# Thirty attention units as a hardware loop with hand-made semaphores, in a decode kernel that streams 572 MB

## The chip, the cores and the metric

The kernel runs on one core of a Trainium2 chip. The metric is device time in microseconds, the median of the runs shown. All other times come from one profiled execution of the same program, read as a page of tables and as answers from its trace.

## The reference

Two branches are computed for two tokens (B = 2, one position each) and mixed by a gate. Branch A is attention of one query over a cache of 16,384 positions in 32 heads of 128; branch B is an MLP with two layer norms. All inputs are bfloat16.

```python
x = A_x                                            # (2, 1, 1024)
g = sigmoid((x * gate_w).sum(-1, keepdims=True))
q = (x @ wq).reshape(B, 1, 32, 128).transpose(0, 2, 1, 3)     # wq: 1024 x 4096
p = softmax(einsum("bhqd,bhkd->bhqk", q, k_cache) * 128 ** -0.5)
a = (p @ v_cache).reshape(B, 1, 4096) @ wo                    # caches: 2 x 32 x 16384 x 128
h = gelu(layernorm(x) @ w1)                                   # w1, w2: 1024 x 1024
x1 = x + shifted(h) @ w2       # shifts along the one position: shifted(h) is zero
b = x1 + gelu(layernorm(x1) @ w3) @ w4                        # w3: 1024 x 3584, w4: 3584 x 1024
out = g * a + (1 - g) * b
```

## The kernel before

The caches are read once. One unit is two heads of one token: 8.39 MB of K and as much of V, each in one transfer of 128 rows of 64 KB. There are 32 units, numbered `n` or `u`; units 2i and 2i+1 are the two tokens of the same pair of heads. On-chip memory has one big tile `mem` of five cells of 32 KB per partition. K of even units lies in cells 0 and 1, K of odd units in cells 1 and 2, and V in cells 3 and 4. `wq`, then `w3`, then `w4` pass through cells 3 and 4 before the first V, and `w1` and `w2` through cell 2.

For each unit DVE transposes K in eight chunks (line 472). PE multiplies each chunk with the unit's query (line 478; 64 matmuls into one PSUM tile `S`). Then come the maximum (499 to 515; DVE, ACT and one PE matmul that brings the maxima to all partitions), the exponentials on ACT (517), and the sum and its reciprocal (531, 533). P.V is done two units later (553; 64 matmuls with 8 weight columns, which run on four groups of 32 rows of the result side by side), with DVE and two PE matmuls to reduce the four groups (569 to 609). After the second token of a pair the result is multiplied with two heads' rows of `wo` (441) into `arow`, a PSUM tile that stays open for the whole kernel.

All large loads go through SP's queue, in this order: `wq`, the two small inputs `xin` and `gwT`, `w1`, `w2`, K of unit 0, the two halves of `w3`, K of unit 1, then in each unit K of the next unit and V of the previous one, and every fourth unit two pairs' rows of `wo` (1 MB). K(n+1) is issued when the first half of unit n has been transposed, since the two share a cell; V(n-1) when P.V of unit n-2 has been read. The last V comes in nine pieces, the last rows of `wo` behind them. In the last units twelve tiny loads of a few rows (`probe`, line 456) go through the same queue.

The MLP and the query use their weights as the stationary operand: `LinearT.compute` (line 233) and line 268 issue one weight load and one matmul with two columns for each 128 x 128 block of a weight matrix: 256 for `wq`, 64 each for `w1` and `w2`, 224 each for `w3` and `w4`. The MLP's result is added into `arow` through 32 matmuls with the identity (line 402) and the output is copied from `arow` by DVE and ACT, a half each (688, 689).

The program is straight code for each engine. A scheduler orders the instructions and makes the semaphores.

Of the kernel before, what the change touches and what calls it, by code (L numbers as in the profile page):

```python
# [19 lines left out]
GELU_C1 = 0.044715  # L20


@with_exitstack
def kernel(
# [21 lines left out]
    assert D % P == 0 and F % P == 0 and H % 2 == 0  # L46
# [4 lines left out]

    HP = H // 2
    NU = HP * B
# [9 lines left out]
    assert NJ % CT == 0 and CT % GT == 0 and NG <= QP  # L63

    const = ctx.enter_context(tc.tile_pool(name="const", bufs=1))
    ktpool = ctx.enter_context(tc.tile_pool(name="ktpool", bufs=2))
    wopool = ctx.enter_context(tc.tile_pool(name="wopool", bufs=1))
    ppool = ctx.enter_context(tc.tile_pool(name="ppool", bufs=1))
    stat = ctx.enter_context(tc.tile_pool(name="stat", bufs=2))
    mlp = ctx.enter_context(tc.tile_pool(name="mlp", bufs=1))  # L70
    sps = ctx.enter_context(tc.tile_pool(name="sps", bufs=2, space=PSUM))
    ops = ctx.enter_context(tc.tile_pool(name="ops", bufs=1, space=PSUM))
    rps = ctx.enter_context(tc.tile_pool(name="rps", bufs=1, space=PSUM))
    mps = ctx.enter_context(tc.tile_pool(name="mps", bufs=2, space=PSUM))

    def misc_psum(shape, dtype=FP32):
        return mps.tile(shape, dtype, tag="misc", name="misc")


    mem = const.tile([P, 5 * CELL], BF16, name="mem")  # L80
# [3 lines left out]

    k_cell = [0 if u % 2 == 0 else 1 for u in range(NU)]
    v_cell = [3] * NU
    v_cell[NU - 2] = 0
    units = [(hp, b) for hp in range(HP) for b in range(B)]

    def cache_rows(cache, u):  # L90
        hp, b = units[u]
        return cache[b, 2 * hp : 2 * hp + 2].rearrange("h s d -> (h s) d").rearrange(
            "(p j) d -> p (j d)", p=P
        )

    def load_k(u):
        nc.sync.dma_start(out=region(k_cell[u], NJ * Dh), in_=cache_rows(A_k_cache, u))

    def load_v(u):
        nc.sync.dma_start(out=region(v_cell[u], NJ * Dh), in_=cache_rows(A_v_cache, u))  # L100

    def load_v_half(u, k):
        at = slice(k * CELL, (k + 1) * CELL)
        nc.sync.dma_start(out=region(v_cell[u], NJ * Dh)[:, at], in_=cache_rows(A_v_cache, u)[:, at])

    PIECES = [32] * 7 + [16] * 2
    assert sum(PIECES) == NJ

    def load_v_pieces(u):
        j = 0  # L110
        for n in PIECES:
            nc.sync.dma_start(
                out=region(v_cell[u], NJ * Dh)[:, j * Dh : (j + n) * Dh],
                in_=cache_rows(A_v_cache, u)[:, j * Dh : (j + n) * Dh],
            )
            j += n

    def k_view(u):
        return region(k_cell[u], NJ * Dh).rearrange("p (j d) -> p j d", d=Dh)

    def v_view(u):
        return region(v_cell[u], NJ * Dh).rearrange("p (j d) -> p j d", d=Dh)

    wq_t = region(3, KC * H * Dh).rearrange("p (r n) -> p r n", r=KC)
    nc.sync.dma_start(out=region(3, KC * H * Dh), in_=A_wq.rearrange("(p r) n -> p (r n)", p=P))
    xin = const.tile([P, B, KC], BF16)
    nc.sync.dma_start(out=xin[:], in_=A_x.rearrange("b s (p r) -> p (b s) r", p=P))
    gwT = const.tile([P, KC], BF16)
    nc.sync.dma_start(out=gwT[:], in_=gate_w.rearrange("(p r) -> p r", p=P))
    ident_f = const.tile([P, P], FP32)  # L130
    make_identity(nc, ident_f[:])
    ident_s = const.tile([P, P], FP32)
    nc.vector.tensor_scalar(
        out=ident_s[:], in0=ident_f[:], scalar1=-scale, scalar2=None, op0=ALU.mult
    )
    neg_half = const.tile([P, 1], FP32)
    nc.vector.memset(neg_half[:], -0.5)
    ones_f = const.tile([P, P], FP32)
    nc.vector.memset(ones_f[:], 1.0)

    sel = const.tile([P, 4, Q4, QP], BF16)
    nc.gpsimd.memset(sel[:], 0.0)
    for v in range(4):
        w, e = divmod(v, 2)
        nc.gpsimd.affine_select(
            out=sel[:, v],
            in_=sel[:, v],
            compare_op=ALU.not_equal,
            fill=1.0,
            base=-(2 * QP * w + e),  # L150
            pattern=[[0, Q4], [-2, QP]],
            channel_multiplier=1,
        )
    mask4 = const.tile([P, Q4], BF16)
    nc.gpsimd.memset(mask4[:], 1.0)
    nc.gpsimd.affine_select(
        out=mask4[:], in_=mask4[:], compare_op=ALU.is_ge, fill=0.0,
        base=0, pattern=[[-QP, Q4]], channel_multiplier=1,
    )
    nc.gpsimd.affine_select(  # L160
        out=mask4[:], in_=mask4[:], compare_op=ALU.is_ge, fill=0.0,
        base=QP - 1, pattern=[[QP, Q4]], channel_multiplier=-1,
    )

    hm2 = const.tile([P, 2], FP32)
    nc.vector.memset(hm2[:], 0.0)
    nc.vector.memset(hm2[0:HALF, 0:1], 1.0)
    nc.vector.memset(hm2[HALF:P, 1:2], 1.0)

    lmat = const.tile([P, P], FP32)  # L170
    nc.vector.tensor_copy(
        out=lmat[:].rearrange("p (g h k) -> p g h k", h=2, k=4),
        in_=hm2[:].unsqueeze(1).unsqueeze(3).to_broadcast([P, P // 8, 2, 4]),
    )

    sel8 = const.tile([P, 8], FP32)
    nc.vector.tensor_reduce(
        out=sel8[:],
        in_=ident_f[:].rearrange("p (c k) -> p k c", k=QP)[:, 0:8, :],
        axis=AX.X,  # L180
        op=ALU.add,
    )

    mask4m = const.tile([P, 4], FP32)
    nc.vector.tensor_tensor(out=mask4m[:], in0=sel8[:, 0:4], in1=sel8[:, 4:8], op=ALU.add)
    hsel = const.tile([P, 2], FP32)
    nc.vector.tensor_reduce(
        out=hsel[:], in_=sel8[:].rearrange("p (h k) -> p h k", k=4), axis=AX.X, op=ALU.add
    )
    oacc = [ops.tile([P, 4 * Dh], FP32, name=f"oacc{k}") for k in range(2)]  # L190
    for k in range(2):
        nc.vector.memset(oacc[k][:], 0.0)

    NW = 2
    WW = P + NG
    qw = []
    for k in range(NW):
        t = const.tile([P, 4, WW], BF16, name=f"qw{k}")
        nc.gpsimd.memset(t[:], 0.0)
        qw.append(t)  # L200
    NP = 4
    pts = []
    for k in range(NP):
        t = const.tile([P, NJ // 4, 2, 4], BF16, name=f"pt{k}")
        nc.gpsimd.memset(t[:], 0.0)
        pts.append(t)

    class LinearT:

        def __init__(self, W, actT, name, cell, offset, nparts=1):  # L210
            self.actT = actT
            K, self.N = W.shape
            self.R = K // P
            self.C = self.N // P
            self.rows = self.R // nparts
            self.src = W.rearrange("(p r) n -> p (r n)", p=P)

            self.at = [(cell + k) * CELL + offset for k in range(nparts)]
            self.acc = mlp.tile([P, self.C, B], FP32, name=f"{name}_acc")

        def part(self, k):
            return mem[:, self.at[k] : self.at[k] + self.rows * self.N]

        def load(self, k=0):
            n = self.rows * self.N
            nc.sync.dma_start(out=self.part(k), in_=self.src[:, k * n : (k + 1) * n])

        def compute(self, k, c0, c1):
            wc = self.part(k).rearrange("p (r n) -> p r n", n=self.N)
            ps = misc_psum([P, c1 - c0, B])  # L230
            for c in range(c0, c1):
                for r in range(self.rows):
                    nc.tensor.matmul(  # L233
                        ps[:, c - c0, :],
                        lhsT=wc[:, r, :].rearrange("p (m c) -> p c m", c=self.C)[:, c, :],
                        rhs=self.actT[:, k * self.rows + r, :],
                        start=(r == 0),
                        stop=(r == self.rows - 1),
                    )
            acc = self.acc[:, c0:c1, :]  # L240
            if k == 0:
                nc.vector.tensor_copy(out=acc, in_=ps[:])
            else:
                nc.vector.tensor_tensor(out=acc, in0=acc, in1=ps[:], op=ALU.add)

    xn1T = mlp.tile([P, KC, B], BF16)
    hT = mlp.tile([P, KC, B], BF16)
    shT = mlp.tile([P, KC, B], BF16)
    x1T = mlp.tile([P, KC, B], FP32)
    xn2T = mlp.tile([P, KC, B], BF16)  # L250
    h2T = mlp.tile([P, FC, B], BF16)
# [137 lines left out]
    def mlp_post4():  # L389
# [10 lines left out]
        for k in range(Q4):  # L400
            for c in range(KC):
# [6 lines left out]
                    skip_group_check=True,  # L408
                )

    OT = const.tile([P, HP, 2, B], BF16)
    LASTP = 2
# [310 lines left out]
```

## Time and profile before

| What | Value |
| --- | --- |
| Median of 3 runs | 1341.56 us (1341.01 to 1341.66) |
| Span of the profiled execution | 1339.6 us |
| Around the span, against the median | 2.0 us |
| PE busy | 770.4 us (58%), 5502 matmuls and 5502 weight loads |
| DVE busy | 705.6 us (53%) |
| ACT busy | 105.1 us (8%) |
| Moved | 573.34 MB, 428 GB/s on average |
| Clock granted to PE, mean | 0.78 |

The three runs lie within 0.65 us of each other. The span is the time from the first to the last instruction of the program in the profiled execution; the runs' times hold a little more at both ends. Busy shares are averages over the whole span. The DMA queues are numbered on the page: q1 is SP's, q10 ACT's, and q8 and q14 carry instructions, that is the code of the program itself, which the engines read from memory while they run. A DMA packet is one contiguous piece that one of the 16 DMA engines moves; the trace lists start, duration and size of each.

### The profile page before, as it was taken

What the parts mean: (1) busy time and instruction counts of PE and PEld (TensorE: products, weight loads), DVE (VectorE), ACT (ScalarE), POOL (GpSimd) and SP (SyncE); (2) the same over time, 40 slices, a digit from 0 to 9 for tenths busy, and PEclk for the clock granted to TensorE, in tenths of its full rate; (3) what the DMA queues carried; (4) which work ended last, traced back from release to release, by engine and by line L of the source; (5) the groups of instructions that cost most, each with busy time, mean ns of one, the idle gap of its engine ahead of it and who ended that gap; (6) DMA issues with size and microseconds to landing.
All of it is one profiled execution on the core that took longest, in us unless ns stands there. A gap on an engine that the chain in (4) does not pass through costs nothing.

```text
span 1339.6 us, 12506 instructions
## 1 busy us (share of the span) xinstructions
PE 770.4 (58%) x5502; PEld 351.5 (26%) x5502; DVE 705.6 (53%) x695; ACT 105.1 (8%) x165; POOL 15.2 (1%) x54
## 2 busy tenths in 40 slices
PE   2679566554566645556654546665455665555564
PEld 2456222221222212222222222222122222222222
DVE  1445566554556555456655545656444665545561
ACT  0011000000000000000000000000000000000000
POOL 1000000000000000000000000000000000000000
PEclk9977888776788767788776778877778887777886
DMA  9999999999999999999999999999999999999997
GB/s 406 425 429 434 438 435 431 435 420 444 425 435 437 435 427 435 423 435 435 437 433 429 427 435 427 425 435 432 437 437 429 425 431 435 425 435 433 433 427 306
DMA packets 14648, 573.34 MB, mean 428 GB/s; under 512 B 2042, under 2 KB 2050, under 8 KB 4610
## 3 DMA queue, kind: packets, MB, share of 16 engines
q1 hardware_dynamic: 14586, 572.54, 99.3%
q8 instruction: 43, 0.70, 0.2%
q14 instruction: 11, 0.09, 0.0%
q10 hardware_dynamic: 8, 0.00, 0.0%
HBM read 572.53 MB, written 0.00 MB: 427 GB/s over the span
## 4 chain that ended last, share of the span: by engine, by line
DMA 67%; PE 16%; DVE 12%; issue 4%; ACT 0%; another core or an unknown queue 0%; POOL 0%; SPq 0%; DVEq 0%; ACTq 0%
DMA mem<-in_A_k_cache_dram 62%; PE S L478 13%; DVE KT L472 12%; PE misc L233 2%; DMA mem<-in_A_v_cache_dram 2%; DMA xin<-in_A_x_dram 2%; DMA wo<-in_A_wo_dram 1%; PE misc L268 1%; ACT pt L517 0%; PE arow L402 0%; PE oacc L553 0%; DVE St L499 0%; POOL ln_rstd L350 0%; PE misc L344 0%
## 5 line engine op out<-in xcount | busy, mean ns | idle before, releaser
L478 PE MATMUL S<-KT,qw 128*128 128x512 bf16 x2048 | 547.2, 417 | 367.6 <-DVE KT L472 367.4
L472 DVE STREAM_TRANSPOSE KT<-mem 128x2048 f32<-128x2048 f32 x256 | 571.3, 2283 | 272.2 <-DMA mem<-in_A_k_cache_dram 218.3
L478 PEld LDWEIGHTS <-qw 128*128 128x128 bf16 x2048 | 218.1, 107 | 688.9 <-issue 511.1
L553 PE MATMUL oacc<-mem,pt 128*8 128x512 bf16 x2008 | 116.4, 383 | 8.9 <-DMA mem<-in_A_v_cache_dram 8.8
L517 ACT ACTIVATE pt<-St,nb 64x256 bf16<-64x256 f32 x64 | 90.0, 1406 | 148.5 <-DVE nb L515 147.6
L503 ACT ACTIVATE Dm<-ident_s,m 128x128 f32<-128x128 f32 x32 | 12.8, 401 | 999.8 <-DVE m L501 999.8
L531 PE MATMUL misc<-rs,lmat 128*128 128x1 f32 x62 | 18.2, 362 | 85.4 <-ACT pt L517 85.3
L553 PEld LDWEIGHTS <-pt 128*8 128x8 bf16 x2008 | 46.3, 87 | 76.1 <-issue 25.5
L499 DVE STREAM_TRANSPOSE St<-S 128x512 f32<-128x512 f32 x32 | 22.9, 717 | 66.5 <-PE S L478 66.5
L533 DVE RECIPROCAL rinv<-misc 128x1 f32<-128x1 f32 x31 | 5.2, 169 | 96.3 <-PE misc L531 96.3
L569 DVE TENSOR_SCALAR part<-oacc,maskr 128x128 f32<-128x128 f32 x31 | 10.9, 351 | 82.7 <-PE oacc L553 82.7
L600 PE MATMUL misc<-hsel,red 128*128 128x2 f32 x112 | 17.1, 257 | 51.5 <-DVE red L575 51.5
L531 PEld LDWEIGHTS misc<-rs,lmat 128*128 128x128 f32 x62 | 15.5, 311 | 93.9 <-ACT pt L517 93.9
L233 PEld LDWEIGHTS <-mem 128*128 128x128 bf16 x576 | 36.9, 169 | 2.2 <-issue 1.4
L600 PEld LDWEIGHTS misc<-hsel,red 128*128 128x128 f32 x112 | 15.5, 198 | 64.8 <-issue 62.6
L517 ACT ACTIVATION_READ_ACCUMULATOR pt<-St,nb 64x1 f32 x64 | 30.7, 479 | 0.0
L575 DVE SCALAR_TENSOR_TENSOR part<-oacc,maskr,part 128x128 f32<-128x128 f32 x62 | 21.8, 351 | 2.2
L268 PE MATMUL misc<-xT,mem 128*128 128x2 bf16 x256 | 7.1, 165 | 26.1 <-DVE xT L263 23.2
L301 POOL TENSOR_TENSOR qw<-qd,mask 128x16 bf16<-128x16 bf16 x32 | 8.4, 264 | 1188.8 <-PE S L478 1160.2
L609 DVE CAST OT<-misc 64x2 bf16<-64x2 f32 x56 | 9.0, 160 | 22.5 <-PE misc L600 22.2
L509 PE MATMUL misc<-Dm,ones_f 128*128 128x128 f32 x64 | 15.7, 330 | 3.5 <-ACT Dm L503 3.5
L515 DVE TENSOR_REDUCE nb<-misc 64x1 f32<-64x64 f32 x64 | 14.2, 222 | 4.9 <-PE misc L509 3.1
(97 smaller groups left out, 150.4 us busy)
## 6 DMA issues: line engine op xcount, KB each, us to landing
mem<-in_B_w_dram SPq DMA_DIRECT2D x4, 3584.0 KB
mem<-in_A_v_cache_dram SPq DMA_DIRECT2D x2, 4096.0 KB
wo<-in_A_wo_dram SPq DMA_DIRECT2D x7, 1024.0 KB
mem<-in_A_v_cache_dram SPq DMA_DIRECT2D x7, 1024.0 KB
mem<-in_B_w_dram SPq DMA_DIRECT2D x2, 2048.0 KB
mem<-in_A_v_cache_dram SPq DMA_DIRECT2D x2, 512.0 KB
wo<-in_A_wo_dram SPq DMA_DIRECT2D x4, 256.0 KB
mem<-in_A_k_cache_dram SPq DMA_DIRECT2D x32
```

Of the source, the lines that this page charges most:

```text
L233: nc.tensor.matmul(ps[:, c - c0, :], lhsT=wc[:, r, :].rearrange("p (m c) -> p c m", c=self.C)[:, c, :], rhs=self.actT[:, k * self.rows + r ...
L268: nc.tensor.matmul(qps[:, h, :], lhsT=wq_t[:, r, h * Dh : (h + 1) * Dh], rhs=xT[:, r, :], start=(r == 0), stop=(r == KC - 1),)
L472: nc.vector.transpose(out=kt[:], in_=Kc.rearrange("p j d -> p (j d)").bitcast(FP32))
L478: nc.tensor.matmul(S, lhsT=t[:, v, NG - 1 - m : NG - 1 - m + P], rhs=ktb[:, half * GT : (half + 1) * GT, w, :, e], start=(first and n == 0 ...
L499: nc.vector.transpose(out=st[:].rearrange("p j r -> p (j r)"), in_=S[:])
L509: nc.tensor.matmul(R_ps[:], lhsT=ones_f[:], rhs=Dm[:], start=True, stop=True)
L515: nc.vector.tensor_reduce(out=nb[rows], in_=R_ps[rows, rows], axis=AX.X, op=ALU.min)
L517: nc.scalar.activation(out=Pt[rows, :, e, :].rearrange("p (m a) k -> p a k m", a=GT // 4), in_=st[rows, :, 0:NG].rearrange("p (a k) m -> p ...
L531: nc.tensor.matmul(tot_ps[:, 0:1], lhsT=lmat[:], rhs=rs[:], start=True, stop=True)
L553: nc.tensor.matmul(acc[QP * q : QP * q + 8, :], lhsT=pts[u % NP][:, g].rearrange("p h k -> p (h k)"), rhs=v_view(u)[:, 4 * g : 4 * g + 4, ...
L575: nc.vector.scalar_tensor_tensor(out=red[:] if twice else part[:], in0=in0.unsqueeze(1).to_broadcast([P, 2, Dh]) if twice else in0, scalar ...
L600: nc.tensor.matmul(ot[:, r, :], lhsT=red[:, r : 2 * Dh : 2], rhs=hsel[:], start=True, stop=True,)
```

## The change

The kernel is written anew with its own semaphores inside one critical section, so that no scheduler orders it. A small class `Line` gives each engine a counting semaphore and each operation the waits that its operands need; it serves the part before the loop. In the loop, counters of finished steps are compared with the round's number, which each engine holds in a register.

- Units 0 and 1 come first, with the MLP between them. Units 2 to 31 are a loop of 15 rounds over all engines, two units per round, with P.V of the two units before. The loads of a round take their place in the caches from the loop's register. There is no barrier at the end of a round.
- The order on PE in one unit is: eight chunks of scores, the matmul of the maxima, P.V of two units before, its reduction, in the second unit the projection with `wo`, then the sum. Before, P.V stood ahead of the matmul of the maxima.
- `wo` is loaded 0.5 MB per round into one tile and no longer 1 MB every second pair; the last pair's 0.5 MB follow the last V in two loads.
- The query and the MLP have the activations as stationary operand (two columns) and the weights moving, in four row groups side by side: 64 matmuls of 512 columns for `wq`, 32 of 256 for each of `w1` and `w2`, 64 of 448 for `w3`, 112 of 256 for `w4`. The results lie as rows and are turned by DVE transposes.
- `w3` and `w4` come in one load each, `V` of unit 0 too. `x`, `gate_w` and a copy of `x` in rows come over ACT's queue. The `probe` loads are gone.
- The MLP's result, times 1 - g, stays in a tile `brow`, and the output is one DVE addition of `arow` and `brow`.

In the built program PE has 2037 instructions, of which the loop has 569; DVE has 184, ACT 53, SP 70 and POOL 47.

```diff
-    for n in range(NU):
-        score_first(n)
-        if n + 1 < NU:
-            load_k(n + 1)
...
-        else:
-            pv(n - 2)
-            if n < NU - 1:
-                load_v(n - 1)
-                load_probes(n)
...
-            pv_end(n - 2)
...
-            softmax_b(n)
-            softmax_c(n)
+        with nc.Fori(1, HP) as i:
+            hi = nc.snap(i + 1)
+            lo16 = nc.snap(i * 16)
+            hi16 = nc.snap(i * 16 + 16)
+            for s in range(2):
+                cells = region(K_CELL[s], NJ * Dh)
+                wait(SP, "tr13" if s == 0 else "tr03", i if s == 0 else hi)
+                SP.dma_start(out=cells, in_=unit_rows(k_rows, i, s)).then_inc(S(f"kl{s}"), 16)
+                wait(SP, f"pvd{1 - s}", i)
+                SP.dma_start(out=region(V_CELL, NJ * Dh), in_=unit_rows(v_rows, i - 1, s)).then_inc(S(f"vl{s}"), 16)
+                if s == 0:
+                    wait(SP, "wod", i)
+                    SP.dma_start(out=wo_t[:].rearrange("p r n -> p (r n)"), in_=wo_source(i - 1)).then_inc(S("wol"), 16)
+            for s in range(2):
+                pool_unit(i, s, hi)
+                act_unit(i, s, hi)
+                dve_scores(i, s, hi, hi16)
+                pe_scores(i, s, hi)
+                pe_pv(i, s, hi, lo16)
+                dve_pv_end(i, s, hi)
+                if s == 1:
+                    pe_project(i, lo16)
+                dve_nb(i, s, hi)
+                pe_tot(i, s, hi)
+                dve_recip(i, s, hi)
...
+        def pe_scores(i, s, hi):
+            wait(PE, f"qwd{s}", hi)
+            wait(PE, f"stT{s}", i)
+            for n, c in enumerate(chunk_ids(s)):
+                wait(PE, f"tr{s}{n}", hi)
...
+                ins.then_inc(S(f"sc{s}{n}"), 1)
+            wait(PE, f"dm{s}", hi)
+            PE.matmul(R_ps[:, 0:P], lhsT=ones_f[:], rhs=Dm[:], start=True, stop=True).then_inc(S(f"rr{s}"), 1)
...
+        def linear(actT, w, R, N, act_key, w_key, banks, out_keys):
+            G = N // Q4
+            width = G // len(banks)
...
+                return PE.matmul(
+                    banks[k][QP * g : QP * g + B, 0:width],
+                    lhsT=actT[:, r, :],
+                    rhs=w[:, r, g * G + k * width : g * G + (k + 1) * width],
...
-    nc.vector.tensor_copy(out=out_row[used, 0:half], in_=arow_t[used, 0:half])
-    nc.scalar.activation(out=out_row[used, half:NQ], in_=arow_t[used, half:NQ], func=ACTF.Copy)
+        DVE.tensor_tensor(out=out_row[used, :], in0=arow_t[used, :], in1=brow[used, :], op=ALU.add).then_inc(S("fin"), 1)
```

More of the change, by code (lines that the diff above doesn't have):

```diff
@@ L70 @@
[L70 to L80, printed above, removed]
+    psum = ctx.enter_context(tc.tile_pool(name="psum", bufs=1, space=PSUM))
@@ new lines @@
+    part = sb([P, Dh], FP32, "part")
+    red = sb([P, 2, Dh], FP32, "red")
+    OT = sb([P, 2, B], BF16, "OT")
+    OTl = sb([P, 2, B], BF16, "OT_last")
+    out_row = sb([P, NQ], BF16, "out_row")
+    sps = [psum.tile([P, GT * QP], FP32, name=f"S{k}") for k in range(2)]
+    oacc2 = psum.tile([P, 2, 4 * Dh], FP32, name="oacc")
+    oacc = [oacc2[:, k, :] for k in range(2)]
+    arow_t = psum.tile([P, NQ], FP32, name="arow")
+    arow = [arow_t[QP * k : QP * k + B, :] for k in range(Q4)]
+    R_ps = psum.tile([P, 2 * P], FP32, name="R")
@@ L160 @@
[L160 to L174, printed above, removed]
@@ L190 @@
[L190 to L206, printed above, removed]
@@ L208 @@
[L208 to L242, printed above, removed]
-            else:
-                nc.vector.tensor_tensor(out=acc, in0=acc, in1=ps[:], op=ALU.add)
@@ new lines @@
+        many(
+            Q4,
+            lambda g: PE.matmul(
+                R_ps[:, g * 64 : (g + 1) * 64],
+                lhsT=rep4[:, g, :],
+                rhs=qTb[:].rearrange("p c b -> p (c b)"),
+                start=True,
+                stop=True,
+                skip_group_check=True,
+            ),
+            ["rep4", "qTb"], ["R"],
+        )
+        for e in range(2):
+            rows = slice(e * HALF, (e + 1) * HALF)
+            ln.op(
+                "DVE",
+                lambda rows=rows, e=e: DVE.tensor_copy(
+                    out=qd[rows],
+                    in_=R_ps[rows].rearrange("p (hp e v b) -> p e hp b v", e=2, v=4, b=B)[:, e],
+                ),
+                reads=["R"], writes=["qd"],
+            )
@@ new lines @@
+        layernorm_T(xT[:], xn1T[:], "ln1", "xT", "xn1T")
+        w1_v = w1_t.rearrange("p (r n) -> p r n", n=D)
+        w2_v = w2_t.rearrange("p (r n) -> p r n", n=D)
+        linear(xn1T, w1_v, KC, D, "xn1T", "w1", [ot_ps[:]], ["ot"])
+        ln.op(
+            "DVE", lambda: DVE.transpose(out=tsc[:, 0:NQ], in_=psum_rows(ot_ps[:], KC)),
+            reads=["ot"], writes=["tsc"],
+        )
+        gelu_T(columns(KC), hT[:], KC, "g1", "hT")
+        many(
+            Q4,
+            lambda g: PE.matmul(
+                arow[g],
+                lhsT=shT[:, 0, :],
+                rhs=rep4[:].rearrange("p g m -> p (g m)")[:, 0:NQ],
+                start=True,
+                stop=False,
+                skip_group_check=True,
+            ),
+            ["shT", "rep4"], ["arow"],
+        )
@@ new lines @@
+        linear(shT, w2_v, KC, D, "shT", "w2", [ot_ps[:]], ["ot"])
+        ln.op(
+            "DVE", lambda: DVE.transpose(out=tsc[:, 0:NQ], in_=psum_rows(ot_ps[:], KC)),
+            reads=["ot"], writes=["tsc"],
+        )
+        ln.op(
+            "DVE", lambda: DVE.tensor_tensor(out=x1T[:], in0=columns(KC), in1=xT[:], op=ALU.add),
+            reads=["tsc", "xT"], writes=["x1T"],
+        )
+        for g in range(Q4):
+            rows = slice(QP * g, QP * g + B)
+            ln.op(
+                "DVE",
+                lambda rows=rows: DVE.tensor_tensor(
+                    out=x1row[rows, :], in0=ot_ps[rows, :], in1=xrow[rows, :], op=ALU.add
+                ),
+                reads=["ot", "xrow0", "xrow1"], writes=["x1row"],
+            )
@@ new lines, in pe_project @@
+        def pe_project(i, lo16):
+            wait(PE, "wol", lo16)
+            for s in range(2):
+                wait(PE, f"OTd{s}", i)
+            for r in range(2):
+                for k in range(Q4):
+                    ins = PE.matmul(
+                        arow[k],
+                        lhsT=OT[:, r, :],
+                        rhs=wo_t[:, r, k * NQ : (k + 1) * NQ],
+                        start=False,
+                        stop=False,
+                        skip_group_check=True,
+                    )
+            ins.then_inc(S("wod"), 1)
@@ new lines @@
+        wo_heads = A_wo.rearrange("(h d) n -> d h n", d=Dh)
+        for e in range(2):
+            SP.dma_start(out=wo_l[:, e, :], in_=wo_heads[:, H - 2 + e, :]).then_inc(S(f"l_wo{e}"), 16)
+        ln.writer.clear()
+        ln.readers.clear()
+        ln.op(
+            "DVE",
+            lambda: DVE.tensor_scalar(out=rs2_t[:], in0=hm2[:], scalar1=rs_t[:, 0:1], scalar2=None, op0=ALU.mult),
+            writes=["rs2"],
+        )
+        many(
+            1, lambda n: PE.matmul(tot_ps[:], lhsT=ones_f[:], rhs=rs2_t[:], start=True, stop=True),
+            ["rs2"], ["tot"],
+        )
@@ new lines @@
+        wait(DVE, "pvd0", HP)
+        dve_rows(0, maskr[0], "pa0", HP).then_inc(S("rd0"), 1)
+        wait(PE, "rd0", HP)
+        PE.matmul(ot_ps[:, 0:2], lhsT=red[:, 0, :], rhs=hsel[:], start=True, stop=True).then_inc(S("otd0"), 1)
+        wait(DVE, "otd0", HP)
+        DVE.tensor_copy(out=OTl[:, :, 0], in_=ot_ps[:, 0:2]).then_inc(S("OTd0"), 1)
+        V = v_view(V_CELL)
+        moving = sum(PIECES[:3])
+        for n in range(3):
+            wait(PE, f"l_v31_{n}", 16)
+            ins = pv_moving(V, 1, n * 8, (n + 1) * 8, moving // 4)
@@ new lines @@
+        ins.then_inc(S("pvd1"), 1)
+        wait(DVE, "pvd1", HP + 1)
+        dve_rows(1, mask4m, "pa1", HP).then_inc(S("rd1"), 1)
+        wait(PE, "rd1", HP)
+        last = R_ps[:, 0:2]
+        PE.matmul(last, lhsT=red[:, 0, :], rhs=hsel[:], start=True, stop=False)
+        j = moving
+        for n in range(3, len(PIECES)):
+            wait(PE, f"l_v31_{n}", 16)
+            for _ in range(PIECES[n]):
+                ins = PE.matmul(
+                    last, lhsT=V[:, j, :], rhs=pts[1][:, j // 4, :, j % 4], start=False, stop=(j == NJ - 1)
+                )
+                j += 1
@@ new lines @@
+        ins.then_inc(S("otd1"), 1)
+        wait(DVE, "otd1", HP)
+        DVE.tensor_tensor(out=OTl[:, :, 1], in0=last, in1=rinv2[:], op=ALU.mult).then_inc(S("OTd1"), 1)
+        wait(PE, "OTd0", HP)
+        wait(PE, "OTd1", HP)
+        for e in range(2):
+            wait(PE, f"l_wo{e}", 16)
+            for k in range(Q4):
+                ins = PE.matmul(
+                    arow[k], lhsT=OTl[:, e, :], rhs=wo_l[:, e, k * NQ : (k + 1) * NQ],
+                    start=False, stop=(e == 1), skip_group_check=True,
+                )
```

1106 lines of the change are left out of this document (639 added, 467 removed).

## The prediction

> **What bounds the kernel now.** I read the page's slices and queues first, then the chain that ended last, one unit's timeline, the last microseconds, and at the end the trace's list of DMA packets.
>
> ```profile
> DMA  9999999999999999999999999999999999999997
> q1 hardware_dynamic: 14586, 572.54, 99.3%
> q8 instruction: 43, 0.70, 0.2%
> DMA 67%; PE 16%; DVE 12%; issue 4%; ACT 0%; another core or an unknown queue 0%; POOL 0%; SPq 0%; DVEq 0%; ACTq 0%
> ```
>
> The 16 DMA engines are full in 39 slices of 40, and the chain is mostly DMA. So time comes from what each DMA engine has to move, from the start, and from the end; PE and DVE count only where they let the queue run dry. One unit shows how far off that is:
>
> ```profile
> 207.88 4.50 DVE L472 STREAM_TRANSPOSE KT<-mem 128x2048 f32<-128x2048 f32 x2 [6.59 <-DMA mem<-in_A_k_cache_dram]
> 218.39 0.33 SPq L97 DMA_DIRECT2D mem<-in_A_k_cache_dram  x1
> 229.02 3.63 PE L553 MATMUL oacc<-mem,pt 128*8 128x512 bf16 x64
> 232.69 0.33 SPq L100 DMA_DIRECT2D mem<-in_A_v_cache_dram  x1
> 238.64 0.59 PE L531 MATMUL misc<-rs,lmat 128*128 128x1 f32 x2 [3.22 <-ACT pt L517]
> 246.58 2.31 DVE L472 STREAM_TRANSPOSE KT<-mem 128x2048 f32<-128x2048 f32 x1 [6.82 <-DMA mem<-in_A_k_cache_dram]
> ```
>
> K lands at 207.9, the next K at 246.6: 38.7 us for two loads, 19.35 each. The next K is queued at 218.4, 9 us before V's transfer ends (227.2); the next V at 232.7, 14 us before K's ends. Compute finishes 7 us early.
>
> ```profile
> 1328.00:1330.00 2.00, 1.01 (x32) 0.93 (x32) 0.00 (x0) 0.00 (x0) 0.00 (x0) 0.50 0.82 323
> 1330.00:1332.00 2.00, 1.25 (x41) 1.18 (x42) 0.00 (x0) 0.00 (x0) 0.00 (x0) 0.50 0.60 237
> 1332.00:1334.00 2.00, 1.27 (x33) 0.93 (x31) 0.16 (x1) 0.00 (x0) 0.00 (x0) 0.50 0.45 166
> 1334.00:1336.00 2.00, 1.18 (x16) 0.27 (x11) 0.00 (x0) 0.00 (x0) 0.00 (x0) 0.50 0.06 24
> ```
>
> These windows (last columns: DMA share, GB/s) show the engines stopping one after another: by the packet list, following packets end to start, the first has its last data at 1328.6, the last at 1335.1, though each moves the same 35.8 MB. What differs is the q8 row, 43 code pages of 16,384 B: 256 instructions of 64 B each, and 43 x 256 = 11,008 against 11,004 PE records (5502 + 5502). A page takes 1.02 to 1.11 us of one DMA engine, and the 65,536 B packet behind it 2.89 to 2.97 us where the median is 2.42: 1.54 us in all. The pages rotate: their durations repeat every eighth (third 1061, 1060, 1068 ns; fourth 1099, 1107, 1099; seventh 1026, 1018, 1018), so eight engines get them, five or six each. The sixteen completions of one load drift apart in step: 2.05 us at 59.6, 5.2 at 480, 6.8 at 714. Six pages are 9.2 us on the engine that ends last. Without them it would end at 1335.1 - 9.2 = 1325.9; the leaders, which end at 1328.6 but ran dry where the spread shrank from 6.8 to 5.9 and from 7.1 to 5.7, give 1328.6 - 2.2 = 1326.4. I take 1326.1.
>
> **The change, part by part.** The profile's time: span 1339.58, and 1.98 around it to the median 1341.56 (the three runs lie within 0.65); I keep the 1.98.
>
> *Loop on PE.* The changed program's instruction list has 2,037 PE instructions, eight pages; the loop body has 569, in three of them (the fourth to the sixth). Fetches are on the path, as just shown. Trace of before never jumps back, so their number is bounded from both sides: if PE's store keeps the pages it has read, each page comes once: two are there at the start (the first q8 packet is at 29.8, after 449 PE records, more than a page) and six are fetched, at most one per engine. If only the current page and the next are kept, each round refetches three and looks ahead to the one behind: 4 x 15 + 4 = 64, eight per engine. I take six, since a rotation over eight looks like eight places for pages, which hold the program; this is a choice and not shown. Slowest engine: 9.2 us become 1.5, so 1326.1 + 1.5 = 1327.6.
>
> [...]
>
> A page also takes time to come: PE stood still for 2.87 us at 29.3, with the fetch packet at 29.76 to 30.84:
>
> ```profile
> 32.20 1.02 PE L268 MATMUL misc<-xT,mem 128*128 128x2 bf16 x33 [2.87 <-issue]
> ```
>
> The page was wanted 256 instructions in, near 26.3, so 6 us; a jump back costs PE between nothing and that. PE ends a unit at 239.2, 7.4 us before the next K lands, and has its first matmul 2.3 after that: hidden. Were it not, the next K's issue has its 9 us.
>
> *Loop order.* SP issues K(n), V(n-2), K(n+1), V(n-1) on the same conditions: first half transposed, P.V done. The wo load waits for the projection a round back, long done. P.V now stands behind the max matmul: S ends +21.2 after K, +0.72 +0.42 +0.40 +0.49 for transpose, max, Dm and matmul, then 3.63: V is queued near +28 instead of +24.8, still 10 us ahead. DVE gets six waits of their own per round, PE three; each between 0 and 0.2 us (DVE's smallest operations take 0.16), under 1 us a unit against 7 of idle. No barrier stands in the loop. Cost nothing; without cover, 1 us a unit.
>
> *q and MLP with weights moving.* q's 256 pairs (6.08 + 1.02 and the stall, 23.3 to 33.2) become 64 matmuls of 512 columns on four row groups; nearest row L553, 64 in 3.63. w3 is queued near 28, not 33.1; K0 lands only at 53.6: worth nothing. w3's matmuls (3.66 + 7.22) become 64 of 448: 3.2. w4 in one load waits for all of them: unit 0's softmax ends near 79.3, so issue near 83 to 86; K1's transfer ends at 53.6 + 17 + 19.35 = 89.9: hidden by 4 us (halves: 83.0 and 90.9). V0 waits for w4's 112 matmuls of 256 columns (3.2, or 6 at half clock), near 119 to 123, against K2's end at 126: hidden by 3. If either cover fails, it costs 1 to 3 us once.
>
> *Transfers.* Per engine, by median packets: w3 and w4 in 57,344 B runs -0.2, V0 whole -0.1, wo in 15 + 1 loads +1.3 - 1.4; twelve probes gone, xin beside the queue: under 0.1. Sum -0.4.
>
> *Start and end.* A branch and a semaphore more before SP's first issue (now 0.79): 0 to +0.6, taken +0.3. At the end:
>
> ```profile
> 1335.62 0.38 PE L441 MATMUL arow<-wo,OT 128*2 128x256 bf16 x4 [0.26 <-DMA wo<-in_A_wo_dram]
> 1336.06 0.29 DVE L688 CAST out_row<-arow 98x128 bf16<-98x128 f32 x1 [2.27 <-PE arow L441]
> 1336.38 0.28 ACT L689 ACTIVATE out_row<-arow 98x128 bf16<-98x128 f32 x1 [33.01 <-DVE out_row L688]
> ```
>
> DVE then ACT, 0.60 from start to end, become one add over 256 columns, 0.4 (0.35 for 128x128 on L569, fewer columns; bound 0.35 to 0.6): -0.2. Leaving the critical section adds a round of engine semaphores, 0 to +0.6, taken +0.3. Last data to end of span, 4.45 now, becomes 4.55.
>
> Sum: 1327.6 - 0.4 + 0.3 + 4.55 = 1332.05, + 1.98 = 1334.0; half of the chance that one engine gets a second page (1.5) makes 1334.8.
>
> **Rivals.**
>
> *Pages do not stay (slower).* 64 fetches, eight per engine: 12.3 us where 9.2 were: 1326.1 + 12.3 - 0.4 + 0.3 + 4.55 + 1.98 = 1344.8, slower by 0.24%; without the look-ahead behind the loop (50, six or seven per engine), 1341.8 to 1343.3, no difference that counts. It turns slower from seven pages on one engine. For it: before never holds more than one page ahead. Against it: the rotation by eight. [...]
>
> *Pages do not stay, and a page always comes by the same engine (much slower).* Four engines get about 16 each: 24.6 us, 1357. Straight code shows the same period of eight for this as for a rotation.
>
> *The count falls, the end does not.* If the drift is the engines' own, or a gate at the start fails by 3 us and the loop gains half, 1339 to 1342. Against it: the drift grows by 1.5 us in steps, with the pages.
>
> **How the numbers follow.** Pages stay: 0.57, 1333 to 1337. Rotating refetch: 0.22, of which slower 0.14, same 0.08 (0.2%, 2.7 us, is about what a measurement of this kernel can tell from no change). Same engine: 0.09, slower. Little change: 0.12, same 0.08, slower 0.04. So faster 0.57, same 0.16, slower 0.27. The range must reach over the rotating refetch: 1332.5 to 1346; the likeliest case alone 1332.5 to 1337.5.
>
> **What would show it.** Right: q8 falls from 43 packets to under 12, the completions of one load stay within 3 us to the end, and the DMA share drops from 1 to 0 within 3 us. Wrong: q8 with 45 packets or more, spaced by rounds; PE idle with "issue" at each jump back; a spread over 8 us; or gaps in the DMA share near 90 or 126, where w4 and V0 are queued late.

## The result, and the profile after

The changed kernel takes 1338.16 us, the median of 11 runs (1336.87 to 1339.08), against 1341.16 us before (11 runs, 1340.88 to 1341.66): a ratio of 0.9976, 95% interval 0.9967 to 0.9985. It is faster, by 3.0 us; the forecast was 1334.8, 6.8 us less than the 1341.56 it started from. The direction held and the time lies within the range, but more than half of the gain is missing. The profiled execution (span 1335.1 us, its run 1336.87) is the fastest of the eleven; why they scatter is part of what follows.

The page of the changed kernel: DMA share in 40 slices, queues (packets, MB, share of the 16 engines) and the chain that ended last.

```profile
DMA  9999999999999999999999999999999999999997
q1 hardware_dynamic: 13544, 572.53, 99.4%
q8 instruction: 8, 0.13, 0.0%
q10 hardware_dynamic: 440, 0.01, 0.0%
DMA 68%; DVE 17%; PE 12%; issue 2%; SPq 0%; ACT 0%; POOL 0%; ACTq 0%; POOLq 0%
```

Code pages fell from 43 to 8. By the packet list six come at 49 to 279 us and two at 1325 and 1329, behind the loop; none in the thousand microseconds between. The kernel is bound as before: DMA full to the last slice.

The last windows of the changed kernel (the last two columns are DMA share and GB/s):

```profile
1326.00:1328.00 2.00, 1.23 (x40) 1.15 (x41) 0.00 (x0) 0.00 (x0) 0.00 (x0) 0.50 0.97 374
1328.00:1330.00 2.00, 1.03 (x35) 0.89 (x31) 0.16 (x1) 0.00 (x0) 0.00 (x0) 0.50 0.30 112
1330.00:1332.00 2.00, 0.64 (x8) 0.11 (x7) 0.42 (x1) 0.00 (x0) 0.00 (x0) 0.50 0.00 0
```

Before, the share ran down over 8 us; now the engines stop within some 2 us, with their last data between 1327.6 and 1329.8 (before: 1328.6 and 1335.1). The sixteen completions of one load lie 2.25 us apart at 247 us and still 2.24 at 1250.

A steady unit of the changed kernel (timeline: start, duration, engine and line, operation, idle time before):

```profile
207.53 4.50 DVE L631 STREAM_TRANSPOSE kt<-mem 128x2048 f32<-128x2048 f32 x2 [4.04 <-DMA mem<-in_A_k_cache_dram]
218.29 0.33 SPq L854 DMA_DIRECT2D mem<-in_A_k_cache_dram  x1
234.79 0.33 SPq L856 DMA_DIRECT2D mem<-in_A_v_cache_dram  x1
```

The next K is queued 10.8 us after K lands, V 27.3 after: the loop's waits and P.V's later place stay under cover, that is, behind a transfer that still runs. What is new lies at 88 us, where `w4` should follow K of unit 1 (K1) in the queue. Timeline, then windows of the changed kernel around it:

```profile
81.86 0.59 PE L697 MATMUL tot<-rs,lmat 128*128 128x1 f32 x2 [3.41 <-ACT pt L674]
82.38 6.00 PE L510 MATMUL oacc<-mem,xn2T 128*2 128x448 bf16 x64
88.49 0.33 SPq L82 DMA_DIRECT2D mem<-in_B_w_dram  x1
```

```profile
84.00:86.00 2.00, 2.00 (x28) 0.66 (x20) 0.00 (x0) 0.00 (x0) 0.00 (x0) 0.50 1.09 467
86.00:88.00 2.00, 2.00 (x28) 0.66 (x20) 0.00 (x0) 0.00 (x0) 0.00 (x0) 0.50 0.24 98
88.00:90.00 2.00, 0.38 (x8) 0.00 (x0) 1.49 (x3) 0.00 (x0) 0.00 (x0) 0.97 1.24 401
90.00:92.00 2.00, 0.00 (x0) 0.00 (x0) 1.58 (x6) 0.25 (x1) 0.00 (x0) 0.88 0.16 57
```

The 64 matmuls of w3 (L510) ran at a granted clock of 0.50 (the third column from the right) and took 6.00 us; w4 waits for them and was queued at 88.49, when K1's transfer had ended on most engines. The four shares sum to 2.73 of 4 (before, in the same windows, to 3.67). By the packet list fourteen of the sixteen engines wait there, for 0.8 to 3.0 us. Part of the lateness is older:

```profile
28.00 0.17 DVE L349 COPY xT<-xin 128x16 bf16<-128x16 bf16 x1 [22.16 <-DMA xin<-in_A_x_dram]
32.98 0.17 DVE L360 TENSOR_TENSOR xg<-xin,gwT 128x16 f32<-128x16 bf16 x1 [4.80 <-DMA gwT<-in_gate_w_dram]
33.93 5.08 PE L510 MATMUL oacc<-mem,xT 128*2 128x512 bf16 x64
39.12 0.33 SPq L82 DMA_DIRECT2D mem<-in_B_w_dram  x1
54.91 4.50 DVE L631 STREAM_TRANSPOSE kt<-mem 128x2048 f32<-128x2048 f32 x2
```

That is the start of the changed kernel: x lands at 28.0 and gate_w at 33.0, on ACT's queue, where before both had landed with wq by 22.5. The same steps before:

```profile
23.02 0.17 DVE L263 COPY xT<-xin 128x16 bf16<-128x16 bf16 x1 [19.27 <-DMA xin<-in_A_x_dram]
53.58 4.51 DVE L472 STREAM_TRANSPOSE KT<-mem 128x2048 f32<-128x2048 f32 x2 [3.68 <-DMA mem<-in_A_k_cache_dram]
83.02 7.85 SPq L226 DMA_DIRECT2D mem<-in_B_w_dram  x2
```

So q, w3's load and both layer norms come late. The last operation of the second layer norm starts at 54.81 on DVE, and unit 0's first transpose, next on that engine, at 54.91 and not at 53.6, although K0 (K of unit 0) was there. (w3 itself loses nothing by being queued at 39.12: its packets start at 51.3, as soon as K0's end.)

### The profile page after: what moved, and what is told of

It reads as the page before. It is cut to its first block, busy times and chain, and to the rows that moved or that the text cites. A ratio compares the mean times of both kernels' runs of the same rounds, so it can differ in the third digit from the quotient of the medians.

```text
span 1335.1 us, 11620 instructions
## 1 busy us (share of the span) xinstructions
PE 752.2 (56%) x4920; PEld 302.5 (23%) x4920; DVE 710.4 (53%) x712; ACT 104.6 (8%) x164; POOL 12.4 (1%) x44
## 3 DMA queue, kind: packets, MB, share of 16 engines
q1 hardware_dynamic: 13544, 572.53, 99.4%
## 4 chain that ended last, share of the span: by engine, by line
DMA 68%; DVE 17%; PE 12%; issue 2%; SPq 0%; ACT 0%; POOL 0%; ACTq 0%; POOLq 0%
DMA mem<-in_A_k_cache_dram 64%; DVE kt L631 16%; PE S L652 11%; DMA gwT<-in_gate_w_dram 2%; DMA mem<-in_A_v_cache_dram 2%; PE oacc L510 1%; PE oacc L702 0%; SPq L879 0%; ACT pt L674 0%; SPq L854 0%; DVE st L636 0%; POOL ln_rstd L450 0%; PE tot L344 0%; DVE tsc L527 0%; DVE tsc L816 0%
## 5 line engine op out<-in xcount | busy, mean ns | idle before, releaser
L652 PE MATMUL S<-kt,qw 128*128 128x512 bf16 x2048 | 547.5, 416 | 303.0 <-DVE kt L631 302.6
L631 DVE STREAM_TRANSPOSE kt<-mem 128x2048 f32<-128x2048 f32 x256 | 570.4, 2282 | 205.0 <-DMA mem<-in_A_k_cache_dram 153.2
L652 PEld LDWEIGHTS S<-kt,qw 128*128 128x128 bf16 x2048 | 195.3, 104 | 642.8 <-issue 335.4
L674 ACT ACTIVATE pt<-st,nb 64x256 bf16<-64x256 f32 x64 | 89.7, 1401 | 226.0 <-DVE nb L688 225.5
L697 PE MATMUL tot<-rs,lmat 128*128 128x1 f32 x64 | 18.7, 362 | 105.4 <-ACT pt L674 105.4
L702 PEld LDWEIGHTS oacc<-mem,pt 128*8 128x8 bf16 x2008 | 46.4, 88 | 61.9 <-issue 4.2
L636 DVE STREAM_TRANSPOSE st<-S 128x512 f32<-128x512 f32 x32 | 23.0, 718 | 64.2 <-PE S L652 64.2
L719 PE MATMUL ot<-hsel,red 128*128 128x2 f32 x120 | 19.0, 263 | 54.7 <-DVE red L756 54.7
L719 PEld LDWEIGHTS ot<-hsel,red 128*128 128x128 f32 x120 | 16.4, 196 | 69.8 <-DVE red L756 69.8
L674 ACT ACTIVATION_READ_ACCUMULATOR pt<-st,nb 64x1 f32 x64 | 30.6, 478 | 0.0
L784 DVE CAST OT<-ot 64x2 bf16<-64x2 f32 x60 | 9.6, 160 | 22.2 <-PE ot L719 21.8
```

The source lines that it names most:

```text
L631: DVE.transpose(out=kt[n % 2][:], in_=k_view(s)[:, c * CT : (c + 1) * CT, :].rearrange("p j d -> p (j d)").bitcast(FP32),).then_inc(S(f"tr ...
L636: DVE.transpose(out=st[:].rearrange("p j r -> p (j r)"), in_=sps[s][:]).then_inc(S(f"stT{s}"), 1)
L652: ins = PE.matmul(sps[s][:].rearrange("p (j k) -> p j k", k=QP), lhsT=qw[s][:, v, NG - 1 - m : NG - 1 - m + P], rhs=ktb[:, half * GT : (ha ...
L674: ins = ACT.activation(out=pts[s][rows, :, e, :].rearrange("p (m a) k -> p a k m", a=GT // 4), in_=st[rows, :, 0:NG].rearrange("p (a k) m ...
L697: PE.matmul(tot_ps[:, 0:1], lhsT=lmat[:], rhs=rs_t[:], start=True, stop=True).then_inc(S(f"tt{s}"), 1)
L702: ins = PE.matmul(oacc[s][QP * q : QP * q + 8, :], lhsT=pts[s][:, g].rearrange("p h k -> p (h k)"), rhs=V[:, 4 * g : 4 * g + 4, :].rearran ...
```

## The experiments

Three questions: is it the code pages, and how many does PE's store keep; what do the lateness at 88 us and x's own lateness cost; and does the sum hold once they are gone. One theory has the fetched pages give all of the gain and the queue, run dry at the start, take half of it back; its rival is that the pages only mark a drift of the engines, and the gain comes from elsewhere.

**The loop written out.** The changed kernel without its loop, all else the same:

```diff
-        with nc.Fori(1, HP) as i:
-            hi = nc.snap(i + 1)
...
+        for i in range(1, HP):
+            hi = i + 1
...
```

> The fifteen rounds written out one after the other, all else as in the changed kernel. PE then has 9911 instructions, 38.7 pages of code. If code pages on the slowest DMA engine set the end: q8 has about 37 packets, four or five per engine on eight engines, 5 x 1.54 = 7.7 us where the loop has 1.5; the sixteen completions of one load drift apart to some 6 us; time 1338.2 + 6.2 = 1344, between 1342 and 1346. If the gain came from the order of work or the semaphores (rival): 1338, whatever q8 shows.

Measured: 1343.37 us (1342.51 to 1346.28), ratio 1.0019 (1.0010 to 1.0028), slower than before. Its page and its last windows:

```profile
q8 instruction: 38, 0.62, 0.2%
```

```profile
1328.00:1330.00 2.00, 1.21 (x48) 1.12 (x45) 0.00 (x0) 0.00 (x0) 0.00 (x0) 1.00 0.98 403
1332.00:1334.00 2.00, 0.88 (x32) 0.80 (x30) 0.00 (x0) 0.00 (x0) 0.00 (x0) 0.50 0.72 282
1336.00:1338.00 2.00, 1.42 (x48) 1.25 (x45) 0.00 (x0) 0.00 (x0) 0.00 (x0) 0.50 0.21 82
1338.00:1340.00 2.00, 1.35 (x24) 0.71 (x24) 0.16 (x1) 0.00 (x0) 0.00 (x0) 0.50 0.04 14
```

The pages and the slow stop are back. The completions of a load again drift apart, from 0.6 us at 52 to 3.9 at 345 and 6.4 at 975. Between 132 and 1320 us no engine waits more than 0.7 us there, so the pages do not act by stopping PE until the queue runs dry. (The profiled run is the slowest of the eleven, 1346.28; waits of up to 2.4 us at 68 and 90 us are in it, too.) By the medians, the loop alone is worth 5.2 us; without it the rest of the change costs 2.1 (before, on the same chip: 1341.25).

**Longer loop bodies.** The same work in loops of five, two and three rounds, so that a lap reads about thirteen, seven and nine pages of PE's code, the one behind the body included (two rounds: round 1 stands ahead of the loop).

```diff
-        with nc.Fori(1, HP) as i:
-            hi = nc.snap(i + 1)
+        with nc.Fori(1, HP - 5 + 1, 5) as first:
+            for k in range(5):
+                i = first if k == 0 else nc.snap(first + k)
+                hi = nc.snap(i + 1)
...
```

> The loop has five rounds in its body and runs three times: 2832 PE instructions from slot 935 to 3767, twelve pages. If PE's store keeps eight pages: each lap reads its pages again, about 40 q8 packets, the time of straight code, 1343 to 1346. If the store keeps sixteen or more: 15 packets, two per engine, 1338 to 1340. If a loop as such, and not its size, brought the gain (rival): 1338.

> Round 1 written out, then a loop with two rounds in its body, seven times: 3166 PE instructions, the loop in slots 1501 to 2632, six pages, seven with the one looked ahead to. If PE's store keeps eight pages: each page comes once, 11 q8 packets, the time of the changed kernel, 1337 to 1340. If it keeps fewer than six (rival): each lap fetches again, 45 packets or more and 1343 to 1346.

> The loop has three rounds in its body and runs five times: slots 935 to 2635, eight pages, nine with the one looked ahead to. If PE's store keeps eight pages and a new one takes the place of the page eight before it: two pages per lap are fetched anew, some 20 q8 packets, 1338 to 1341. If the store keeps more than eight (rival): 11 packets and the time of the changed kernel; if it keeps the eight last read and drops the oldest: all pages each lap, 43 packets and 1343 to 1346.

Measured: five rounds 1344.53 us (1343.96 to 1345.02; ratio 1.0024, 1.0014 to 1.0033); two rounds 1338.68 and three rounds 1344.78 in one run each. The q8 rows of their pages, five, two and three rounds in turn:

```profile
q8 instruction: 42, 0.69, 0.2%
```

```profile
q8 instruction: 12, 0.20, 0.1%
```

```profile
q8 instruction: 48, 0.79, 0.2%
```

With seven pages a lap nothing is fetched between 355 and 1316 us: the first lap brings the pages, six more laps find them. With nine, each of the five laps fetches nine. So the store holds seven and not nine (12 packets over seven laps, 48 over five), and with nine a lap every page goes before it is used again. No run shows a cost of the jump back itself.

The times follow from the page counts within 1.1 us, with the prediction's price of 1.54 us for each page and eight engines to share them (two and three rounds are one run each, against a changed kernel whose own runs lie 2.2 us apart):

| Kernel | q8 packets | worked out over the changed kernel | measured |
| --- | --- | --- | --- |
| two rounds | 12 | 4/8 x 1.54 = +0.8 us | +0.5 |
| written out | 38 | 30/8 x 1.54 = +5.8 | +5.2 |
| five rounds | 42 | 34/8 x 1.54 = +6.5 | +6.4 |
| three rounds | 48 | 40/8 x 1.54 = +7.7 | +6.6 |

**w3's matmuls early.** They stand ahead of the matmul of unit 0's maxima, and no longer behind its softmax.

```diff
+            if s == 0:
+                linear(xn2T, w3_v, KC, F, "xn2T", "c3", [oacc[0], oacc[1]], ["oacc0", "oacc1"])
+                pe_max(0, 1)
...
-        linear(xn2T, w3_v, KC, F, "xn2T", "c3", [oacc[0], oacc[1]], ["oacc0", "oacc1"])
```

> w3's 64 matmuls stand ahead of unit 0's matmul of the maxima on PE instead of behind its softmax; all else as in the changed kernel. If w4 was queued too late (88.5 us, when the queue had run dry for 1.3 to 3.0 us on each DMA engine): w4 is queued near 82.5, no gap near 88, 2 to 3 us faster, 1335 to 1336.3, and the runs lie closer together. If the gap has another cause, or its time is lost later anyway (rival): 1338.

Measured: 1335.94 us (1335.41 to 1336.71), ratio 0.9962 (0.9948 to 0.9976), 2.2 below the changed kernel. w4 is queued at 78.97 and no engine waits for it; now V0 (V of unit 0), queued at 123.26, comes late, and single engines wait up to 1.6 us near 124.

**x and gate_w ahead of wq on SP's queue.**

```diff
+        ln.dma("SP", xin[:], ...)
+        ln.dma("SP", gwT[:], ...)
         ln.dma("SP", region(3, KC * H * Dh), A_wq...)
...
-        ln.dma("ACT", xin[:], ...)
-        ln.dma("ACT", gwT[:], ...)
```

> x and gate_w come over SP's queue ahead of wq instead of over ACT's queue; all else as in the changed kernel. If x landing at 28 and gate_w at 33 us held up q, the layer norms and with them unit 0 (transposes at 54.9 where K was there at 53.6): q starts when wq lands, near 22 to 24, w3 is queued near 30, unit 0 begins 1.3 us earlier, w4 is queued near 87.1, the gap shrinks by as much: 1336.5 to 1337.5. If unit 0 does not wait for that chain (rival): 1338, with w4 queued at 88.5 as before.

Measured: 1338.08 us (1335.82 to 1339.03), ratio 0.9974 (0.9965 to 0.9983): no gain over the changed kernel, where 0.7 to 1.7 were expected. The second layer norm now ends at 45.05, 10 us earlier, but wq was queued at 1.97 instead of 0.97, so that K0, too, came later (first transpose 54.41). The wait near 88 shrank to at most 2.4 us on a few engines, and one of at most 2.7 opened at 125.

**w4 in two loads**, the first when half of w3 has been read: the part "single load" undone alone.

```diff
-        linear(xn2T, w3_v, ...)
-        ln.dma("SP", region(3, FC * D), w_rows[3], "l_w4", writes=["c3"])
+        for n, key in enumerate(("c3a", "c3b")):
+            linear(xn2T, w3_v, ..., rows=range(n * KC // 2, (n + 1) * KC // 2))
+            ln.dma("SP", region(3, FC * D)[:, at], w_rows[3][:, at], f"l_w4{n}", writes=[key])
```

> w4 comes in two halves, the first queued when w3's first four rows have been read, as before the change; all else as in the changed kernel. If the single load is what made w4 late: first half queued near 85.5 (88.5 less half of w3's 6 us), the gap near 88 all but closed; but V of unit 0 is then late near 125, as in e4_x_first, where the gap only moved: 1336.5 to 1338. If the two gates were independent (rival): 1335.5 to 1336.2.

Measured: 1337.65 us (1335.99 to 1340.02), ratio 0.9977 (0.9967 to 0.9987). The first half is queued at 85.54, 3 us sooner, and most of the wait moves to 124, where V0 is queued at 124.14. The interval is that of the changed kernel: two loads in place of one, alone, gain nothing that these runs can tell.

**Both sets of matmuls early**, w3's and w4's, each ahead of its unit's matmul of the maxima:

```diff
+            else:
+                linear(h2T, w4_v, FC, D, "h2T", "c3", [ot_ps[:]], ["ot"])
...
+            pe_max(s, 1)
```

> As e3_w3_early, and w4's 112 matmuls stand ahead of unit 1's matmul of the maxima instead of behind its softmax, so that V of unit 0 can be queued sooner. If the two late loads at the start (w4 near 88, V of unit 0 near 124) are the whole loss against the forecast apart from the end: V queued near 118, no gap above 0.3 us besides code pages on any DMA engine, 0.5 to 1.5 us below e3: 1334.4 to 1335.4. If nothing waits at 124 that counts (rival): as e3, 1335.9.

Measured: 1334.92 us (1334.40 to 1336.77), ratio 0.9953 (0.9939 to 0.9966). Its profiled run was the slowest, and shows why: q's matmuls took 6.20 us there, the second layer norm ended later, unit 0 began at 55.78 and K1 was queued at 66.56; several engines waited up to 2.0 us near 68. That is a third place where x's lateness reaches the queue.

**x and gate_w behind wq**, as before the change; alone, and with both sets of matmuls early:

```diff
         ln.dma("SP", region(3, KC * H * Dh), A_wq...)
+        ln.dma("SP", xin[:], ...)
+        ln.dma("SP", gwT[:], ...)
...
-        ln.dma("ACT", xin[:], ...)
-        ln.dma("ACT", gwT[:], ...)
```

> The changed kernel, with xin and gwT issued on SP's queue directly behind wq, where they stood before, and no longer on ACT's queue; w4's matmuls stay in their place. Theory: their 16 B packets then land with wq near 22.5 and not at 28 to 33; the second layer norm ends before K0 lands, unit 0's first transpose starts at 53.4 to 53.8 (54.9 in the changed kernel), and everything up to w4's issue moves forward by 1.1 to 1.4 us: w4 queued near 87.2 in place of 88.5. The gap of 1.3 to 3.0 us near 88 shrinks to at most 1.8, and V0, still late at 123, opens one of up to 2.5 near 125, since w4 then ends earlier: the time gains 0.3 to 1.3, 1336.9 to 1337.9. Rival (x's late arrival costs nothing, the gap near 88 is the matmuls at half clock alone): the time stays at 1338.2 and unit 0 starts as late as before the edit.

> Both edits: w3's and w4's matmuls ahead of the matmul of the maxima, and xin and gwT on SP's queue behind wq. In the profiled run of the version with the early matmuls alone (1336.77, where its other runs were 1334.4 to 1335.5) K1 was queued at 66.56 and up to 2 us of DMA time were lost near 68, since unit 0 started at 55.8. Theory: with x behind wq unit 0 starts at 53.4 to 53.8 in every run, K1 is queued near 64.2, no engine waits near 68, 88 or 125, and the time is 1333.8 to 1334.6 with runs within 1 us of each other. Rival (the scatter comes from something else): the median stays at 1334.9 and single runs still reach 1336 to 1337.

Measured: alone 1336.48 us (1335.62 to 1337.40), ratio 0.9963 (0.9949 to 0.9977); together 1334.55 (1334.46 to 1334.78), ratio 0.9950 (0.9936 to 0.9963). The timeline of x behind wq alone:

```profile
23.20 0.17 DVE L349 COPY xT<-xin 128x16 bf16<-128x16 bf16 x1 [17.37 <-DMA xin<-in_A_x_dram]
53.74 4.50 DVE L631 STREAM_TRANSPOSE kt<-mem 128x2048 f32<-128x2048 f32 x2 [7.16 <-DMA mem<-in_A_k_cache_dram]
81.33 4.82 PE L510 MATMUL oacc<-mem,xn2T 128*2 128x448 bf16 x64
86.26 0.33 SPq L82 DMA_DIRECT2D mem<-in_B_w_dram  x1
```

w4 is queued 2.2 us sooner: 1.05 because w3's matmuls start sooner, 1.2 because they ran 4.82 us and not 6.00 in this execution. The gain of 1.7 is above the 0.3 to 1.3 that were expected; that x's place costs nothing is out. With both edits, timeline and windows:

```profile
75.59 3.20 PE L510 MATMUL oacc<-mem,xn2T 128*2 128x448 bf16 x64
78.89 0.33 SPq L82 DMA_DIRECT2D mem<-in_B_w_dram  x1
111.29 3.23 PE L510 MATMUL ot<-mem,h2T 128*2 128x256 bf16 x112
114.81 0.34 SPq L863 DMA_DIRECT2D mem<-in_A_v_cache_dram  x1
```

```profile
84.00:86.00 2.00, 0.00 (x0) 0.00 (x0) 1.51 (x7) 0.25 (x1) 0.00 (x0) 0.50 1.13 492
86.00:88.00 2.00, 0.00 (x0) 0.00 (x0) 0.14 (x1) 0.00 (x0) 0.00 (x0) 0.50 0.96 414
88.00:90.00 2.00, 0.00 (x0) 0.00 (x0) 0.00 (x0) 0.00 (x0) 0.00 (x0) 0.50 1.00 430
90.00:92.00 2.00, 0.00 (x0) 0.00 (x0) 1.71 (x1) 0.00 (x0) 0.00 (x0) 0.50 0.86 373
```

w4 and V0 are queued 9.6 and 9.2 us sooner than in the changed kernel. Unit 0 starts at 53.98 and K1 is queued at 64.95, a little later than expected, and no engine waits near 68. The four shares sum to 3.95 where they were 2.73, and by the packet list no engine waits longer than 0.3 us but for a code page. This version is faster than both kernels, by 6.7 us than the one before, and its runs lie within 0.32 us of each other, where those of the changed kernel lay within 2.2. So the scatter came from the late steps at the start.

## Why the prediction was right, and where it was not

A cover is the time by which a load is queued ahead of the end of the transfer before it. The last column is the version with both sets of matmuls early and x behind wq. The sum, term by term, for one profiled execution each (the last row: all runs):

| | predicted | changed kernel | both covers restored |
| --- | --- | --- | --- |
| last data | 1327.5 | 1329.8 | 1327.6 |
| last data to end of span | 4.55 | 5.3 | 5.3 |
| around the span | 1.98 | 1.8 | 1.9 |
| that run | 1334.0 | 1336.9 | 1334.8 |
| median | 1334.8 | 1338.16 | 1334.55 |

**Code pages: right.** The forecast took 43 pages as the cause of the slow stop, priced a page at 1.54 us and chose a store of eight. The count, the constant spread and the quick stop follow, and the times at 12, 38, 42 and 48 pages do within 1.1 us; the last data of the version with covers, 1327.6, is the sum's 1327.5. Eight pages came and not six: two lie behind the loop. The rivals with refetches did not come true: that PE keeps only the current page and the next is not what it shows, since a loop over three pages and the one behind brought no fetch between 279 and 1325 us. But refetching as such is real, with nine pages a lap, and makes the kernel slower. That this gave 1344.78 where the forecast had 1344.8 for its rival is chance: the forecast counted 64 fetches and no late load, the run had 48 and w4 queued late, at 88.21.

**w4's cover: failed, and this is the missing gain.** The step put w4's issue "near 83 to 86", hidden by 4 us; it came at 88.49. Three terms were mis-sized. w3's matmuls were put at 3.2 us and took 6.00 at half clock, an allowance that the step made for w4 alone; in the versions where they follow the scores without a break they took 3.20 at a clock of 1.00. And "xin beside the queue: under 0.1" priced the bytes and not the moment of landing: 5.5 us later for x, 10.5 for gate_w, so that w3 was queued at 39.1 and not near 28, and unit 0 began 1.3 us late. And the cover's far end, 89.9, is the end of K1 on the last engine alone: by the packet list thirteen of the sixteen end it between 87.5 and 88.1 and the last at 89.5, while w4's first packet starts 1.0 us behind its issue (89.46). So on most engines the cover ended near 86.5 to 87.1 and not at 89.9, hardly behind the "83 to 86" of the forecast; had all engines ended K1 at 89.9, an issue at 88.49 would have cost nothing. The price that the text gave for a lost cover, 1 to 3 us once, is near what was lost: 2.3 in the profiled run, the fastest of the eleven, and 3.6 between the medians of the changed kernel and of the version with covers. The sign that it named, a gap in the DMA share near 90, is the one that showed.

**V0's cover: thin, as told.** V0 came at 123.97, one later than "119 to 123":

```profile
118.77 4.90 PE L510 MATMUL ot<-mem,h2T 128*2 128x256 bf16 x112
123.97 0.34 SPq L856 DMA_DIRECT2D mem<-in_A_v_cache_dram  x1
```

In the changed kernel no engine waits there, since w4 was itself late and pushed K2 (K of unit 2) back. Where w4 alone was repaired, a wait for V0 opened in its place. The two losses do not add; that is the likely reason why moving x alone to the head of the queue, or halving w4, gained next to nothing.

**The end: one term right, one too small.** The merged output took 0.42 us from start to end where DVE and ACT took 0.60: -0.2, as worked out.

```profile
1330.69 0.42 DVE L952 TENSOR_TENSOR out_row<-arow,brow 98x256 bf16<-98x256 f32 x1 [0.85 <-PE arow L945]
1331.14 0.66 SPq L955 DMA_DIRECT2D out_dram<-out_row  x1
```

Leaving the critical section was put at +0.3, with no row behind that figure. From the last output packet (1332.8) to the end of the span (1335.1) it takes 2.3 us, and 2.3 in every other version but the one with two rounds in the body (2.8), against 1.3 before: +1.0. No run separates what in that exit takes the time, since dropping its waits alone was not tried; it stays open. The start cost +0.18 (first issue 0.97, was 0.79), put at +0.3, again with no row behind it. So it is in part luck that the last row of the table agrees so well: the forecast of 1334.8 adds 0.8 to its sum for a second page on one engine, and the end takes 0.75 more than the sum has.

**The loop's order: right.** V was put at +28 behind K's landing (the terms named add up to 26.9) and came at +27.3; the jump back leaves no late K. DVE's smallest operations are shorter than the 0.16 us of the text (0.06, a memset of 128 x 1), which changes nothing under a cover of 7 us.

**The third rival**, "a gate at the start fails by 3 us and the loop gains half", 1339 to 1342 with little change, comes nearest to the measured time, 1 us too high, and its first half is what happened. The second half is not: the loop brought 5.2 us where the page counts give 5.8. It was given 0.12; its evidence was in the forecast itself, in two covers of 3 and 4 us over steps of which one was already known to take 3.2 or 6.

## What to carry to other kernels

Where every DMA engine is full (99.4% for SP's queue here), count what else it must carry: here 43 code pages of 16 KB cost 1.54 us for each page on the engine that ends last, and a loop whose body fits PE's store left 8 of them (12 with two rounds in the body), while one round too many in the body (three, not two) brought 48. A cover of 3 us over a step of matmuls that may run at half clock is no cover (w3's took 6.00 us at 0.50), and it ends with the first engine that runs dry, not with the last (K1 ended at 87.5 and 89.5); put such matmuls right behind other matmuls (3.20 us at 1.00), and price a small load by when it lands, not by its bytes (x landed 5.5 us later on ACT's queue).

## What the runs showed of the hardware

**Tiny packets on a second queue wait for a large one each.** In the changed kernel a DMA engine takes in turns one 16 B packet of ACT's queue and one packet of SP's. On one engine, followed packet by packet, the 16 B packets start at 5.32, 7.74, 10.16, 12.58 and so on, 2.42 us apart as long as SP's are 64 KB, and 0.61 apart behind the 16 KB packets of w1 and w2; 24 of them end at 31.5. On SP's queue behind wq, the same packets all run between 21.8 and 22.6 (before) or 21.9 and 22.7 (the experiment).

**PE's code store.** Seven pages of 16 KB stay over a lap (12 packets in all, over seven laps) and nine do not (48, over five); at nine none is left when its turn comes again. Whether it holds eight, no run separates.

**The clock after a pause.** The same 64 matmuls of 448 columns took 3.20 us right behind the scores, at a granted clock of 1.00, and 6.00 after 6 us (76 to 82) in which PE was busy for 0.84, at 0.50. In the other versions with that pause they took between 4.8 and 6.2, and the clock came back during them at different times: its mean was 0.83 over 84 to 86 us with x behind wq alone, 1.00 over 86 to 88 with two rounds in the body, and in the changed kernel still 0.50 there and 0.97 over 88 to 90.
